# Reciprocals of token sums in two halves of the heads, each with its own store and broadcast, and their minimum and sum taken once, in a gated mix of a recurrent-memory transformer and an MLP

## The chip, the cores and the metric

The kernel runs on one core of a Trainium2 chip. The metric is the device time of one launch in microseconds (us), taken as the median of several runs. Engines are named as in the profile: PE (TensorE) with PEld, its weight loads, DVE (VectorE), ACT (ScalarE), POOL (GpSimd) and SP (SyncE), which issues most of the DMAs.

## The reference

Two branches read the same input x of 2048 tokens by 512 features, and a gate mixes them:

```python
g = _sigmoid((x * gate_w).sum(-1, keepdims=True))
a = _A_ref(x, A_mem0, A_Wq, A_Wk, A_Wv, A_Wo, A_seg_len)
b = _B_ref(x, B_w1, B_b1, B_w2, B_b2)
return g * a + (1 - g) * b
```

Branch B is a layer norm, a matmul to 1376 features, a tanh GELU and a matmul back. Branch A is a recurrence over 64 segments of 32 tokens. Each segment's input is 8 memory rows followed by its 32 tokens, 40 rows in all. The rows are projected to queries, keys and values of 32 heads with 128 features each. Scores are masked (token rows see the memory and earlier tokens, memory rows see everything), go through a softmax and weigh the values, and the output projection Wo gives 40 rows of 512. The last 32 are the segment's output, and the first 8 are the memory of the next segment. So segments cannot run side by side: each needs the 8 memory rows of the one before.

## The kernel before, in words

The whole kernel is written under a manual schedule: the order in which instructions are written is the order on each engine, and waits are derived from which tiles (and which PSUM banks) they share.

First comes branch B over 16 tiles of 128 tokens, in 8 blocks of two, while the weights of branch A are loaded. Its result, times 1 - g, goes to DRAM (`c_dr`). This takes about the first 96 us. Then comes the loop over 64 segments, `for s in range(nseg)` (L665), where s counts segments, T = s // 4 the tile of 128 tokens and si = s % 4 the place in it.

The 40 rows of a segment are split so that one matmul group has 32: 24 of its tokens with the 8 memory rows (`hT`), while the other 8 tokens ("left") of four segments are handled together for the next tile, since they don't need the memory. That left work, and the output sums, are the filler between steps of the recurrence; `run(n)` takes n pieces of it. Heads are kept as eight groups i of four, j = 0 to 3, one j for each 32 rows of the PE array. "Half 0" is the head groups i = 0 to 3, "half 1" is 4 to 7.

One segment, with the lines that the prediction uses:

- Four projections of queries and keys (L122) into the PSUM banks U, cast by ACT (L127) and transposed by DVE (L131) into QT and KT. One of the filler's is also L122, into the banks X.
- `scores` of half 0 into the bank SbF (L259, L263), one exponential on ACT (L713), values (L141, cast at L719), then the sums of half 0: `xsums` (L616) sums the exponentials of the 32 token columns into eight columns of SbF called `xs8`, and `msum` (L270, L273) sums those of the memory rows into bank U. `mnorm(0)` on DVE takes the reciprocal of the memory sums (L709, written into SbF) and multiplies it into E (L710).
- The same for half 1, in the bank W: scores, exponentials (L702, two pieces), `msum(1)`, `mnorm(1)`; later, after some filler, `xsums(E, 1)`.
- `recip_x(s)` (L625): DVE takes the reciprocal of all eight columns of `xs8` (L627) into the last eight columns of the tile R. SP stores them to DRAM (L630, 4 KB) and broadcasts them from there to all 128 partitions as `Rb` (L631, 512 KB). DVE copies the memory reciprocals into R (L633) and writes the mask into SbF again (L252). POOL adds R to the running sum `racc` (L635). DVE takes the running minimum `rmin` at the end of the segment (L766).
- `av` (L283 with the main values, L288 with the left ones): half 0 of the heads, then half 1, into the four U banks. The memory columns are cast into UT at once (L746). The token columns are copied without their normalization (`x_raw`, L622).
- `wo_pass` (L153, 32 matmuls into W) reads UT, which holds the memory columns of this segment and the normalized token columns of the segment before. `new_mem` (L659, L661) turns its result into the next segment's memory rows.
- `x_norm(s - 1)` (L638), written at the head of segment s, is where POOL multiplies the raw token columns by `Rb`: two multiplies into UT and two into UL, for each half of the heads one (L643). `Rb` has one buffer.

SP's queue holds, in program order: loads of c, VP (L182) and the transposed x at the head of a segment, then the store L630, the broadcast L631, and the stores of output tiles (L233).

`racc` and `rmin` are a check on the exponentials, which are taken without subtracting a maximum: after the loop their total over the columns (L794, L795) is compared with two limits (L797, L798), a matmul counts the partitions that are good (L810), and if one is not, a slow path recomputes branch A. With these inputs it isn't entered.

The last segment has no `xsums` and no `recip_x`. It normalizes the token columns directly with a reciprocal of 256 columns (L777) into the same tile R.

Of the kernel before, what the change touches and what calls it, by code (L numbers as in the profile page):

```python
# [27 lines left out]
def kernel(ctx, tc, A_x, A_mem0, A_Wq, A_Wk, A_Wv, A_Wo, A_seg_len, B_x, B_w1, B_b1, B_w2, B_b2, gate_w, out):  # L28
    nc = tc.nc
# [35 lines left out]
    r_dr = [dram.tile([P, NG], FP32, name=f"r_dr{i}") for i in range(2)]  # L65
# [228 lines left out]
    with tc.tile_pool(name="mlpw", bufs=1) as mlpw, \  # L294
# [44 lines left out]
        m0 = ep.tile([M, Dm], BF16)  # L339
# [228 lines left out]
    UL = [lp.tile([P, 4, NG, 32], BF16, name=f"UL{i}") for i in range(2)]  # L568
    racc = lp.tile([P, NG * 40], FP32)
# [40 lines left out]
    RW = 9 * NG  # L610
# [13 lines left out]

    def recip_x(s):  # L625
        R = Rs.pop(s)
        nc.vector.reciprocal(out=R[:, 8 * NG:RW], in_=xs8)  # L627

        Rb = cw.tile([P, P, NG], FP32, tag="Rb", bufs=1, name="Rb")
        nc.sync.dma_start(r_dr[s % 2][:], R[:, 8 * NG:RW])  # L630
        nc.sync.dma_start(Rb[:].rearrange("p r e -> p (r e)"), r_dr[s % 2][:].rearrange("r e -> (r e)").partition_broadcast(P))  # L631
# [6 lines left out]
    def x_norm(s):  # L638
        T, si = divmod(s, SPT)
        XR, Rb = XRs.pop(s), Rbs.pop(s)[:].rearrange("p (c q) (h j) -> p h j c q", c=4, h=2)  # L640
        for out, o, a, b in ((UT[(s + 1) % 2], M, LEFT, 32), (UL[T % 2], LEFT * si, 0, LEFT)):
            for h in range(2):
                nc.gpsimd.tensor_tensor(out=out[:, :, 4 * h:4 * h + 4, o:o + b - a], in0=XR[:, :, 4 * h:4 * h + 4, a:b], in1=Rb[:, h, :, :, a:b], op=ALU.mult)  # L643
# [21 lines left out]
    for s in range(nseg):  # L665
# [30 lines left out]
        R = cw.tile([P, NG * 40], FP32, tag="R", name="R")  # L696
# [26 lines left out]
        if not last:  # L723
            xsums(E, 0)
            msum(0)
            mnorm(0)
# [43 lines left out]
    nx = slice(8 * NG, 40 * NG)  # L770
    sums(xsum, E, 8, 0, 32, True)
# [5 lines left out]
    nc.vector.reciprocal(out=R[:, nx], in_=SbF[:, 0:32 * NG])  # L777
    ws[s - 1] = wo_pass(UT[s % 2])
    Rr = R[:, nx].rearrange("p (i q) -> p i q", q=32)
# [10 lines left out]
    nc.vector.tensor_tensor(out=rmin[:, nx], in0=rmin[:, nx], in1=R[:, nx], op=ALU.min)  # L790
    nc.vector.tensor_tensor(out=racc[:, nx], in0=racc[:, nx], in1=R[:, nx], op=ALU.add)
    okp = loop.enter_context(tc.tile_pool(name="okp", bufs=1))
    tot = okp.tile([P, 2], FP32)
    nc.vector.tensor_reduce(out=tot[:, 0:1], in_=rmin[:], axis=AX.X, op=ALU.min)  # L794
    nc.vector.tensor_reduce(out=tot[:, 1:2], in_=racc[:], axis=AX.X, op=ALU.add)  # L795
# [146 lines left out]
```

## Time and profile before

| what | value |
|---|---|
| median of 3 runs | 769.83 us (769.66 to 770.79) |
| span of the profiled execution | 768.4 us |
| instructions | 43822 |
| TensorE clock granted | 9 tenths or more in all 40 slices |
| DMA | 70.58 MB, mean 92 GB/s |

The span is what the profile covers of one execution; the runs' times hold a little more than that, 1.4 us by the median. "Busy" is the time in which an engine had an instruction; ends of matmuls are modelled, so the start times of matmuls say more than their ends. An idle stretch is put down to the instruction or DMA whose semaphore came last. Where an engine waits for several, the name is a guess, and it is wrong where the engine named had long been done.

### The profile page before, as it was taken

What the parts mean: (1) busy time and instruction counts of PE and PEld (TensorE: products, weight loads), DVE (VectorE), ACT (ScalarE), POOL (GpSimd) and SP (SyncE); (2) the same over time, 40 slices, a digit from 0 to 9 for tenths busy, and PEclk for the clock granted to TensorE, in tenths of its full rate; (3) what the DMA queues carried; (4) which work ended last, traced back from release to release, by engine and by line L of the source; (5) the groups of instructions that cost most, each with busy time, mean ns of one, the idle gap of its engine ahead of it and who ended that gap; (6) DMA issues with size and microseconds to landing.
All of it is one profiled execution on the core that took longest, in us unless ns stands there. A gap on an engine that the chain in (4) does not pass through costs nothing.

```text
span 768.4 us, 43822 instructions
## 1 busy us (share of the span) xinstructions
PE 753.4 (98%) x19186; PEld 412.2 (54%) x19186; DVE 396.1 (52%) x1428; ACT 540.0 (70%) x1631; POOL 278.2 (36%) x522
## 2 busy tenths in 40 slices
PE   7999999999999999999999999999999999999996
PEld 5666554555555555555555555555555555555553
DVE  5776355445445454545554554545454555444444
ACT  4666676777777777777777777777777777777763
POOL 4111033433344443334434334443424443343341
PEclk9999999999999999999999999999999999999999
DMA  6779422223222222212131322122222213122221
GB/s 196 274 233 400 153 58 63 76 63 87 65 59 66 79 72 73 80 53 74 58 89 62 90 63 79 45 80 73 80 72 59 76 49 89 62 83 64 72 67 38
DMA packets 53319, 70.58 MB, mean 92 GB/s; under 512 B 21306, under 2 KB 43043, under 8 KB 51587
## 3 DMA queue, kind: packets, MB, share of 16 engines
q1 hardware_dynamic: 51394, 64.84, 26.8%
q8 instruction: 152, 2.49, 1.4%
q0 software_dynamic: 784, 1.97, 0.8%
q10 hardware_dynamic: 944, 0.92, 0.3%
q14 instruction: 45, 0.36, 0.2%
HBM read 56.96 MB, written 4.45 MB: 80 GB/s over the span
## 4 chain that ended last, share of the span: by engine, by line
PE 96%; DMA 1%; DVE 1%; ACT 1%; issue 0%; SPq 0%; POOL 0%; DVEq 0%; ACTq 0%
PE U L122 30%; PE X L141 18%; PE W L153 15%; PE X L122 7%; PE U L468 4%; PE U L283 4%; PE X L153 4%; PE W L462 2%; PE SbF L462 2%; PE U L270 1%; PE W L259 1%; DMA w_sb<-in_B_w_dram 1%; PE U L659 1%; PE SbF L259 1%; PE SbF L616 1%; PE U L288 1%
## 5 line engine op out<-in xcount | busy, mean ns | idle before, releaser
L643 POOL TENSOR_TENSOR UT<-XR,Rb 128x384 bf16<-128x384 bf16 x126 | 140.3, 1136 | 301.7 <-DMA Rb<-r_dr 220.5
L127 ACT CAST Tb<-U 128x512 bf16<-128x512 f32 x258 | 151.2, 586 | 78.4 <-PE U L122 78.1
L122 PEld LDWEIGHTS <-hT 128*32 128x32 bf16 x4096 | 104.5, 96 | 103.9 <-DVE hT L661 8.6
L141 PE MATMUL X<-Wv_sb,hT 128*32 128x512 bf16 x2048 | 143.8, 378 | 0.0
L122 PE MATMUL U<-Wq_sb,hT 128*32 128x512 bf16 x2048 | 136.1, 381 | 0.3 <-DVE hT L661 0.2
L122 PE MATMUL U<-Wk_sb,hT 128*32 128x512 bf16 x2048 | 132.7, 379 | 0.0
L153 PE MATMUL W<-Wo_sb,UT 128*32 128x512 bf16 x2080 | 124.6, 380 | 1.2 <-POOL racc L635 1.2
L661 DVE CAST hT<-U 128x8 bf16<-128x8 f32 x126 | 20.9, 167 | 172.8 <-PE U L659 163.6
L719 ACT CAST V<-X 128x256 bf16<-128x256 f32 x256 | 88.7, 372 | 14.5 <-PE X L141 0.8
L131 DVE STREAM_TRANSPOSE QT<-Tb 128x256 f32<-128x256 f32 x128 | 57.0, 446 | 76.5 <-ACT Tb L127 76.5
L153 PEld LDWEIGHTS <-UT 128*32 128x32 bf16 x2080 | 57.8, 96 | 56.5 <-issue 13.1
L650 ACT CAST w<-W 128x128 bf16<-128x128 f32 (+1 forms) x192 | 46.0, 311 | 48.2 <-PE W L153 48.2
L622 ACT CAST XR<-U 128x256 bf16<-128x256 f32 x252 | 78.4, 434 | 0.0
L131 DVE STREAM_TRANSPOSE KT<-Tb 128x256 f32<-128x256 f32 x128 | 57.0, 445 | 28.0 <-ACT Tb L127 23.5
L643 POOL TENSOR_TENSOR UL<-XR,Rb 128x128 bf16<-128x128 bf16 x126 | 60.3, 502 | 0.0
L141 PEld LDWEIGHTS <-hT 128*32 128x32 bf16 x2048 | 46.4, 94 | 21.0
L635 POOL TENSOR_TENSOR racc<-racc,R 128x72 f32<-128x72 f32 x63 | 21.3, 338 | 93.4 <-PE U L288 84.1
L468 PE MATMUL U<-w_sb,hTm 128*128 128x512 bf16 (+1 forms) x176 | 52.4, 381 | 0.0
L746 ACT CAST UT<-U 128x64 bf16<-128x64 f32 x252 | 35.4, 226 | 22.9 <-PE U L288 22.8
L462 PEld LDWEIGHTS <-w_sb 128*128 128x128 bf16 (+1 forms) x352 | 34.5, 102 | 20.1 <-issue 1.3
L702 ACT ACTIVATE E<-W 128x64 bf16<-128x64 f32 (+1 forms) x128 | 35.0, 273 | 11.3 <-PE W L263 11.3
L659 PEld LDWEIGHTS <-w 128*32 128x32 bf16 x1008 | 22.8, 93 | 37.2 <-ACT w L650 29.3
(159 smaller groups left out, 1204.7 us busy)
## 6 DMA issues: line engine op xcount, KB each, us to landing
Rb<-r_dr SPq DMA_DIRECT2D x63, 512.0 KB, 3.8
Wv_sb<-in_A_Wv_dram SPq DMA_DIRECT2D x4, 1024.0 KB, 6.3
Wq_sb<-in_A_Wq_dram SPq DMA_DIRECT2D x4, 1024.0 KB, 7.1
Wk_sb<-in_A_Wk_dram SPq DMA_DIRECT2D x4, 1024.0 KB, 9.4
Wo_sb<-in_A_Wo_dram SPq DMA_DIRECT2D x4, 1024.0 KB, 15.0
VP<-VL SPq DMA_DIRECT2D x64, 64.0 KB, 3.5
c<-c_dr SPq DMA_DIRECT2D x16, 128.0 KB, 3.6
xt<-in_A_x_dram SPq DMA_DIRECT2D x15, 128.0 KB, 3.1
```

The lines of the kernel that those rows point to most:

```text
L122: nc.tensor.matmul(bk[32 * j:32 * j + 32, :], lhsT=G[:, kc, :], rhs=W5[t][:, kc, h0:h1, j, :], start=(kc == 0), stop=(kc == KC - 1), tile_ ...
L127: nc.scalar.copy(out=Tb[:], in_=bk.rearrange("p (a b e) -> p a e b", a=8, b=2))
L131: nc.vector.transpose(out=dst[:, 8 * hf:8 * hf + 8, c0:c0 + 32, :].rearrange("p a r b -> p a (r b)").bitcast(FP32), in_=Tb[:].rearrange("p ...
L141: nc.tensor.matmul(bk[32 * j:32 * j + 32, :], lhsT=G[:, kc, :], rhs=Wv5[:, kc, 4 * vb:4 * vb + 4, j, :], start=(kc == 0), stop=(kc == KC - ...
L153: nc.tensor.matmul(bk[32 * c:32 * c + 32, :], lhsT=U_[:, j, i, :], rhs=Wo_sb[:, 4 * i + j, :], start=(n == 0), stop=(n == NW - 1), tile_po ...
L462: nc.tensor.matmul(hp[:rows, 0:TB * P], lhsT=w1_sb[:, kc, fc * P:fc * P + rows], rhs=yTs[blk][:, kc, :], start=(kc == 0), stop=(kc == KC - 1))
L468: nc.tensor.matmul(bp(blk, tt)[:], lhsT=hTm[blk % 2][:rows, fc, tt * P:(tt + 1) * P], rhs=w2_sb[:rows, fc, :], start=(fc == 0), stop=(fc = ...
L622: nc.scalar.copy(out=XR[:, j], in_=U[j][:, 0:NG * 40].rearrange("p (i q) -> p i q", q=40)[:, :, 0:32])
L643: nc.gpsimd.tensor_tensor(out=out[:, :, 4 * h:4 * h + 4, o:o + b - a], in0=XR[:, :, 4 * h:4 * h + 4, a:b], in1=Rb[:, h, :, :, a:b], op=ALU ...
L650: nc.scalar.copy(out=w[:, a:b], in_=W[:, a:b])
L719: nc.scalar.copy(out=V[:, i0:i0 + 2, :].rearrange("p i e -> p (i e)"), in_=(X1, X2)[vb][:, 256 * h:256 * h + 256])
L746: nc.scalar.copy(out=UT[s % 2][:, j, :, 0:M], in_=U[j][:, 0:NG * 40].rearrange("p (i q) -> p i q", q=40)[:, :, 32:40])
```

## The change

R loses the eight columns for the token sums. A new tile RX keeps the reciprocals of all 63 segments, eight columns each. They are taken in two pieces: half 0 right after `msum(0)`, ahead of `mnorm(0)` on DVE, and half 1 where L627 was. Each piece has its own store to its own DRAM tile, and each DRAM tile its own broadcast into its own `Rb` tile; both broadcasts are written in `recip_x`, behind the second store. The running sum and minimum keep the 64 columns of memory sums alone; those of the token sums are taken once after the loop, with two reductions over all 504 columns of RX, and they join the check as second operands of its two comparisons. The reciprocal of the last segment gets a tile of its own. One small tile (m0) moves to the pool of branch B.

```diff
-    r_dr = [dram.tile([P, NG], FP32, name=f"r_dr{i}") for i in range(2)]
+    r_dr = [[dram.tile([P, NG // 2], FP32, name=f"r_dr{i}{h}") for h in range(2)] for i in range(2)]
...
-        m0 = ep.tile([M, Dm], BF16)
+        m0 = mlpw.tile([M, Dm], BF16)
...
+    RX = lp.tile([P, nseg - 1, NG], FP32)
...
-    RW = 9 * NG
+    RW = 8 * NG
...
+    def recip_half(s, h):
+        r = RX[:, s, 4 * h:4 * h + 4]
+        nc.vector.reciprocal(out=r, in_=xs8[:, 4 * h:4 * h + 4])
+        nc.sync.dma_start(r_dr[s % 2][h][:], r)
+
     def recip_x(s):
+        recip_half(s, 1)
         R = Rs.pop(s)
-        nc.vector.reciprocal(out=R[:, 8 * NG:RW], in_=xs8)
-
-        Rb = cw.tile([P, P, NG], FP32, tag="Rb", bufs=1, name="Rb")
-        nc.sync.dma_start(r_dr[s % 2][:], R[:, 8 * NG:RW])
-        nc.sync.dma_start(Rb[:].rearrange("p r e -> p (r e)"), r_dr[s % 2][:].rearrange("r e -> (r e)").partition_broadcast(P))
+        Rb = []
+        for h in range(2):
+            Rb.append(cw.tile([P, P, NG // 2], FP32, tag=f"Rb{h}", bufs=1, name="Rb"))
+            nc.sync.dma_start(Rb[h][:].rearrange("p r e -> p (r e)"), r_dr[s % 2][h][:].rearrange("r e -> (r e)").partition_broadcast(P))
...
-        XR, Rb = XRs.pop(s), Rbs.pop(s)[:].rearrange("p (c q) (h j) -> p h j c q", c=4, h=2)
+        XR, Rb = XRs.pop(s), [r[:].rearrange("p (c q) j -> p j c q", c=4) for r in Rbs.pop(s)]
...
-                nc.gpsimd.tensor_tensor(out=out[:, :, 4 * h:4 * h + 4, o:o + b - a], in0=XR[:, :, 4 * h:4 * h + 4, a:b], in1=Rb[:, h, :, :, a:b], op=ALU.mult)
+                nc.gpsimd.tensor_tensor(out=out[:, :, 4 * h:4 * h + 4, o:o + b - a], in0=XR[:, :, 4 * h:4 * h + 4, a:b], in1=Rb[h][:, :, :, a:b], op=ALU.mult)
...
-        R = cw.tile([P, NG * 40], FP32, tag="R", name="R")
+        R = cw.tile([P, RW], FP32, tag="R", name="R")
...
             xsums(E, 0)
             msum(0)
+            recip_half(s, 0)
             mnorm(0)
...
+    okp = loop.enter_context(tc.tile_pool(name="okp", bufs=1))
+    R = okp.tile([P, 32 * NG], FP32)
+    tot = okp.tile([P, 2, 2], FP32)
+    xr = RX[:].rearrange("p s e -> p (s e)")
+    nc.vector.tensor_reduce(out=tot[:, 0, 0:1], in_=xr, axis=AX.X, op=ALU.min)
+    nc.vector.tensor_reduce(out=tot[:, 1, 0:1], in_=xr, axis=AX.X, op=ALU.add)
...
-    nc.vector.reciprocal(out=R[:, nx], in_=SbF[:, 0:32 * NG])
+    nc.vector.reciprocal(out=R[:], in_=SbF[:, 0:32 * NG])
...
-    nc.vector.tensor_scalar(out=good[:, 0:1], in0=tot[:, 0:1], scalar1=R_MIN, scalar2=None, op0=ALU.is_gt)
-    nc.vector.tensor_scalar(out=good[:, 1:2], in0=tot[:, 1:2], scalar1=RSUM_MAX, scalar2=None, op0=ALU.is_lt)
+    nc.vector.tensor_scalar(out=good[:, 0:1], in0=tot[:, 0, 1:2], scalar1=tot[:, 0, 0:1], scalar2=R_MIN, op0=ALU.min, op1=ALU.is_gt)
+    nc.vector.tensor_scalar(out=good[:, 1:2], in0=tot[:, 1, 1:2], scalar1=tot[:, 1, 0:1], scalar2=RSUM_MAX, op0=ALU.add, op1=ALU.is_lt)
```

12 lines of the change are left out of this document (5 added, 7 removed).

## The prediction

> **What bounds the kernel now.** I read the page first: busy time by engine, then the chain that ended last.
>
> ```profile
> PE 753.4 (98%) x19186; PEld 412.2 (54%) x19186; DVE 396.1 (52%) x1428; ACT 540.0 (70%) x1631; POOL 278.2 (36%) x522
> ```
> ```profile
> PE 96%; DMA 1%; DVE 1%; ACT 1%; issue 0%; SPq 0%; POOL 0%; DVEq 0%; ACTq 0%
> ```
>
> TensorE is the bound. The edit touches VectorE, GpSimd, SyncE's queue and DMA, so it can change the time only where one of these ends a wait of TensorE. Next come the waits: GpSimd's largest, then the two of TensorE's that lie in the loop.
>
> ```profile
> POOL UT L643 <- DMA Rb<-r_dr: 220.5, 45, 6.2
> ```
> ```profile
> PE U L659 <- ACT w L650: 1.5, 4, 0.4
> PE W L153 <- POOL racc L635: 1.2, 3, 0.4
> ```
>
> The change works on the first of these, 220.5 us of GpSimd waiting for the broadcast `Rb`. It is large, but TensorE is not waiting behind it: its only wait that names GpSimd is 1.2 us in 3 places. A busy TensorE hides short stalls, since ends of matmuls are modelled, so I went on to the start times of one segment of 10 us, by engine: VectorE, ScalarE, TensorE, GpSimd, and SyncE's queue.
>
> ```profile
> 401.51 0.37 DVE L709 RECIPROCAL SbF<-U 128x32 f32<-128x32 f32 x1 [0.34 <-ACT V L719]
> 401.91 0.22 DVE L710 TENSOR_TENSOR E<-E,SbF 128x64 bf16<-128x64 bf16 x1
> 402.37 0.37 DVE L709 RECIPROCAL W<-U 128x32 f32<-128x32 f32 x1 [0.24 <-ACT E L702]
> 402.77 0.22 DVE L710 TENSOR_TENSOR E<-E,W 128x64 bf16<-128x64 bf16 x1
> 402.97 0.21 DVE L627 RECIPROCAL R<-SbF 128x8 f32<-128x8 f32 x1
> ```
> ```profile
> 402.02 0.32 ACT L702 ACTIVATE E<-W 128x160 bf16<-128x160 f32 x1
> ```
> ```profile
> 401.10 0.20 PE L616 MATMUL SbF<-BO,E 128*32 128x4 bf16 x8
> 401.15 0.18 PE L270 MATMUL U<-E,BO 128*32 128x32 bf16 x4
> 401.18 0.18 PE L273 MATMUL U<-E,BO 128*32 128x32 bf16 x4
> ...
> 402.77 0.30 PE L283 MATMUL U<-E,V 32*128 32x40 bf16 x16
> 402.89 0.21 PE L288 MATMUL U<-E,VP 32*128 32x64 bf16 x4
> 403.05 0.29 PE L283 MATMUL U<-E,V 32*128 32x40 bf16 x16
> ...
> 403.77 1.91 PE L153 MATMUL W<-Wo_sb,UT 128*32 128x512 bf16 x32
> ```
> ```profile
> 399.78 2.24 POOL L643 TENSOR_TENSOR UT<-XR,Rb 128x384 bf16<-128x384 bf16 x2 [5.97 <-DMA Rb<-r_dr]
> ```
> ```profile
> 403.21 0.33 SPq L630 DMA_DIRECT2D r_dr<-R  x1
> 404.66 0.32 SPq L631 DMA_DIRECT2D Rb<-r_dr  x1
> 405.07 0.53 SPq L182 DMA_DIRECT2D VP<-VL  x1
> ```
>
> Columns: start, duration, engine, line, then in brackets the idle time and what ended it. Two things are to be seen. First, the attention-times-V matmuls follow VectorE closely: the first L283 starts at 402.77, 0.03 after the second L709 reciprocal ends (402.37 + 0.37 = 402.74), the second at 403.05, 0.06 after the second L710 multiply ends (402.99). So **the second normalization sets TensorE's pace, and it starts 0.03 after ScalarE's exponential ends** (402.02 + 0.32 = 402.34). Ahead of it VectorE idled 0.24. Second, GpSimd's `UT` is done at 402.02 and read at 403.77: **1.75 us of reserve**. The tightest segment that I found:
>
> ```profile
> 452.09 2.23 POOL L643 TENSOR_TENSOR UT<-XR,Rb 128x384 bf16<-128x384 bf16 x2 [6.15 <-DMA Rb<-r_dr]
> ```
> ```profile
> 455.25 1.91 PE L153 MATMUL W<-Wo_sb,UT 128*32 128x512 bf16 x32
> ```
>
> Here 455.25 - 454.32 = 0.93 us are left. The broadcast is never what TensorE waits for in this execution.
>
> **The change part by part.** The sum is made against the profiled execution's span, 768.4 us; the median of the runs shown is 769.83, so 1.4 us lie around the span and I add them unchanged. There are 63 segments with the changed work (the last has none).
>
> ```profile
> L709 DVE RECIPROCAL W<-U 128x32 f32<-128x32 f32 x63 | 23.1, 367 | 16.3 <-ACT E L702 12.0 <-PE X L141 3.9 <-PE U L273 0.4
> ...
> L627 DVE RECIPROCAL R<-SbF 128x8 f32<-128x8 f32 x63 | 13.1, 207 | 0.1
> ```
>
> 1. *The reciprocal of half 0, added ahead of the first L709.* 24 columns fewer take 160 ns less (367 to 207), 6.7 ns a column, so four columns take about 180 ns; bounds 0 and the 367 of the 128x32 row, and 207 is the nearest. It reads the L616 sums, which leave TensorE 0.05 to 0.08 before the L273 sums that the first L709 waits for, so it starts about 0.05 earlier than 401.51. The first L709 writes the same bank and waits for its end, plus the 0.03 seen between L709 and L710 (401.88 to 401.91). Queued behind it on VectorE are both normalizations. They move by 0.18 + 0.03 - 0.05 = 0.16 (0.19 with 207). The second L709 had 0.24 idle here and 16.3 / 63 = 0.26 in the mean, and its start is set by ScalarE. Cost **0**; 0.05 to 0.08 of cover remain, and each 10 ns beyond cost 0.63 us. The matmuls of half 1's sums also wait for the first L710, whose end moves to about 402.3; they come after the second L709 has started.
>
> 2. *The reciprocal of half 1*, in the place of L627: four columns for eight, 27 ns less, behind the second normalization, with nothing of TensorE behind it soon. 0. Its old wait for GpSimd moves to the copy that follows; the instruction waited for is two segments old.
>
> 3. *Two stores and two broadcasts* instead of one each, all on SyncE's queue in the order store 0, store 1, broadcast 0, broadcast 1.
>
> ```profile
> r_dr<-R SPq DMA_DIRECT2D x63, 4.0 KB, 1.5
> ```
> ```profile
> DMA to landing us min/median/max: 3.3/3.8/5.6
> ```
>
> Store 0 can go at about 401.7 and lands by 403.2; store 1 goes at 403.2 as before; broadcast 0 at about 403.5 instead of 404.66; broadcast 1 at 404.7, when store 1 has landed. Half 0 arrives about 1.1 us earlier, half 1 with half the bytes at about the old time. 63 x 2 more DMAs take 0.33 of SyncE's queue each; behind them stands the VP load (405.07), which the next segment needs some 10 us after the L288 at 402.89, so a third of a us there costs nothing. GpSimd's four multiplies keep their sizes; two may start earlier, into 1.75 us of reserve that nobody uses. Gain **0**. [...] The 4 KB store here lands in 1.5, and SyncE issues the VP load 0.41 after the broadcast, long before that has landed. [...]
>
> 4. *Minimum and sum once at the end.* L635 on GpSimd and L766 on VectorE lose 8 of 72 columns each; neither has TensorE behind it. Two reductions over 504 columns are added before the last reciprocal:
>
> ```profile
> 752.76 0.45 DVE L131 STREAM_TRANSPOSE KT<-Tb 128x256 f32<-128x256 f32 x1 [0.36 <-ACT Tb L127]
> 755.05 1.76 DVE L777 RECIPROCAL R<-SbF 128x256 f32<-128x256 f32 x1 [1.85 <-ACT V L719]
> ...
> 760.62 0.47 DVE L795 TENSOR_REDUCE tot<-racc 128x1 f32<-128x320 f32 x1
> ```
>
> In proportion 0.47 x 504 / 320 = 0.74 each, 1.5 together, within 1.85 of idle. Uncovered they would cost at most 1.5 once. The two checks keep their number; a second operand from memory in each is 0 within hundredths. Cost 0. The two tiles that move in memory change no wait that is still open when it is reached.
>
> **Sum**: 768.4 + 0 + 1.4 = **769.8 us**.
>
> **The rivals.**
>
> *VectorE becomes late (slower).* If the added reciprocal holds the first L709 for more than 0.24, the second L709 starts late, and L283 with it. At the upper bound, 0.37 + 0.03 - 0.05 = 0.35, so 0.11 x 63 = 6.9: 776.7. For it: the chain is tight and repeated 63 times. Against: the 128x8 reciprocal took 0.21.
>
> *The pair of broadcasts lands later (slower).* Two transfers share one queue and have packets half as long. If each pair ended as late as the slowest broadcast of this trace, 5.6 instead of 3.8, `UT` would be 1.8 later, 0.05 beyond the reserve of 1.75, times 62 = 3.1: 772.9. It decides from 0.93 late in the tightest segment on. Against: half 1's transfer is half as large.
>
> *The irregular stalls go (faster).* Every fourth segment has the same work, so equal spacing is expected. The chain in order of time:
>
> ```profile
> 106.81 3.45 PE U L122 x64
> ...
> 604.50 3.45 PE U L122 x64
> ...
> 645.75 3.45 PE U L122 x64
> ```
>
> Four segments took 41.25 at 604.50, but 497.69 / 12 = 41.47 before that: 12 x 0.22 = 2.7 us of irregular stalls, the 1.2 after GpSimd among them. If the new timing removed all, 767.1. Nothing ties them to the broadcast: `UT` was ready 0.93 or more ahead.
>
> *The change doesn't do what it says*: broadcast 0 stands behind store 1 in the queue, and if it then waits on as before, nothing arrives earlier. The time is again 769.8, since earliness is not used.
>
> **How the numbers follow.** Forecast, with the last rival in it, 0.74, its own range 768.3 to 771.3; the stalls go 0.10; late broadcasts 0.08; late VectorE 0.08. The bound for no change is 0.2%, about 1.5 us, roughly what a measurement of this kernel can tell. Faster 0.10, same 0.74, slower 0.16. The range from 768.3 to 772.9 takes in the forecast and the late broadcasts, 0.82.
>
> **What would show it.** Right: the second L709 still starts 0.03 after L702 ends, its idle falls from 0.26 to about 0.1, L283 keeps its place, GpSimd's wait for `Rb` falls from 220.5 by some 40 to 70 while TensorE's busy time stays near 753, four clean segments take 41.25. Wrong: idle before the second L709 gone and named by VectorE itself, a `UT` that ends after its L153 could start, the KT transpose to last reciprocal stretch at the end longer, or four clean segments off 41.25 by more than 0.1.

## The result and the profile after

The changed kernel took 778.19 us in the median (776.17 to 779.33, 4 runs) beside 770.31 for the kernel before (4 runs): a ratio of 1.0093, 95% interval 1.0074 to 1.0112. Run once more, later, it took 779.30 (1.0107, 1.0090 to 1.0123). It is slower by about 8 us, where 769.8 was forecast and 772.9 was the upper end. The profiled span went from 768.4 to 776.3 us.

Of the changed kernel's page, the lines that answer to those of before: busy time by engine, the chain by engine, and of the DMA queues SyncE's (q1) and the one that brings instructions (q8; packets, MB, share of the time of the 16 DMA engines).

```profile
PE 759.4 (98%) x19186; PEld 418.7 (54%) x19186; DVE 407.0 (52%) x1493; ACT 539.7 (70%) x1631; POOL 278.1 (36%) x522
...
q1 hardware_dynamic: 69538, 64.85, 31.3%
q8 instruction: 152, 2.49, 1.6%
...
PE 95%; DVE 2%; ACT 1%; issue 1%; DMA 1%; POOL 0%; DVEq 0%; ACTq 0%; POOLq 0%
```

The same two queues in the kernel before:

```profile
q1 hardware_dynamic: 51394, 64.84, 26.8%
q8 instruction: 152, 2.49, 1.4%
```

TensorE has the same 19186 matmuls and is "busy" 6.0 us longer (753.4 to 759.4). The change gave it no more work, so this busy time holds pauses too short or too unlike a wait to be shown as idle. The bytes on q1 are equal to 0.01 MB, but they come in a third more packets and hold the DMA engines for 31.3% of the span instead of 26.8%; the instruction queue, with the same 152 packets, went from 1.4 to 1.6%.

The waits of the changed kernel that the change touches (engine, tile and line, what it waited for: us in total, times, longest):

```profile
POOL UT L649 <- DMA Rb<-r_dr: 254.9, 101, 5.2
...
POOL UT L649 <- ACT Tb L127: 27.2, 7, 4.7
...
DVE RX L628 <- PE U L273: 18.2, 62, 0.6
...
ACT E L708 <- DVE RX L628: 10.2, 52, 0.2
...
PEld L122 <- issue: 4.0, 9, 0.6
...
PE W L153 <- ACT UT L753: 1.2, 3, 0.4
```

And in the kernel before:

```profile
POOL UT L643 <- ACT Tb L127: 81.2, 18, 5.9
...
PEld L122 <- issue: 1.8, 5, 0.4
```

GpSimd's wait for `Rb` did not fall, it rose by 34 us; what fell is its wait for `Tb` (81.2 to 27.2), so that both together went from 301.7 to 282.1. The wait changed its name more than its size. Two lines stand out. ScalarE's exponentials now name the added reciprocal. And TensorE's weight loads of L122, in the middle of the projection, sat longer behind "issue", a wait for nothing that the profile shows: 4.0 us in 9 places instead of 1.8 in 5.

One segment of the changed kernel by start times, first VectorE, ScalarE and TensorE around the normalizations:

```profile
404.53 0.20 PE L617 MATMUL SbF<-BO,E 128*32 128x4 bf16 x8
...
404.89 0.18 DVE L628 RECIPROCAL RX<-SbF 128x4 f32<-128x4 f32 x1 [0.55 <-PE U L273]
...
405.11 0.22 ACT L708 ACTIVATE E<-W 128x64 bf16<-128x64 f32 x1 [0.20 <-DVE RX L628]
405.18 0.37 DVE L715 RECIPROCAL SbF<-U 128x32 f32<-128x32 f32 x1
...
405.48 0.32 ACT L708 ACTIVATE E<-W 128x160 bf16<-128x160 f32 x1
405.58 0.22 DVE L716 TENSOR_TENSOR E<-E,SbF 128x64 bf16<-128x64 bf16 x1
...
405.84 0.36 DVE L715 RECIPROCAL W<-U 128x32 f32<-128x32 f32 x1
...
406.23 0.29 PE L283 MATMUL U<-E,V 32*128 32x40 bf16 x16
```

The second L715 starts 0.04 after ScalarE's exponential (405.48 + 0.32 = 405.80) and 0.04 after VectorE's own multiply, which ends at 405.80 too. Before, VectorE had been free 0.24 earlier. From the start of the sums' matmuls (404.53) to the second reciprocal it takes 1.31 here; it took 1.27 before (401.10 to 402.37).

SyncE's queue in that segment, GpSimd's multiplies ahead of it, and the pass that reads `UT`:

```profile
405.10 1.81 SPq L629 DMA_DIRECT2D r_dr<-RX  x2
...
407.02 2.79 SPq L637 DMA_DIRECT2D Rb<-r_dr  x2
...
409.87 0.54 SPq L182 DMA_DIRECT2D VP<-VL  x1
```
```profile
400.28 1.12 POOL L649 TENSOR_TENSOR UT<-XR,Rb 128x384 bf16<-128x384 bf16 x1 [3.46 <-DMA Rb<-r_dr]
400.38 1.10 DVE L773 TENSOR_TENSOR rmin<-rmin,R 128x64 f32<-128x64 f32 x1
...
402.22 1.13 POOL L649 TENSOR_TENSOR UT<-XR,Rb 128x384 bf16<-128x384 bf16 x1 [0.82 <-DMA Rb<-r_dr]
...
403.30 0.28 PE L259 MATMUL SbF<-QT,KT 128*32 128x40 bf16 x16
```
```profile
407.27 1.91 PE L153 MATMUL W<-Wo_sb,UT 128*32 128x512 bf16 x32
```

`UT` is ready at 403.35 and read at 407.27: 3.9 us of reserve, where the segment of the prediction had 1.75. This segment gains more than most. Over all 63 the median reserve went from 2.8 to 3.1 us and the smallest from 0.9 to 1.8, and nobody uses it. The two broadcasts did not come as planned either: counted from the last sums matmul of half 0, the first is issued at 2.78 us and the second at 4.84 (medians), where the single one was at 3.63. The first is earlier, the second later. And one row says what was not foreseen: the running minimum L773 beside GpSimd's first multiply took 1.10 us; alone it takes 0.22. The groups show that this is no rule of the kernel but a few places:

```profile
L715 DVE RECIPROCAL SbF<-U 128x32 f32<-128x32 f32 x63 | 23.1, 366 | 7.0 <-DVE RX L628 0.8
L715 DVE RECIPROCAL W<-U 128x32 f32<-128x32 f32 x63 | 23.0, 366 | 3.3 <-ACT E L708 0.8 <-PE U L273 0.3
L628 DVE RECIPROCAL RX<-SbF 128x4 f32<-128x4 f32 x126 | 22.9, 182 | 18.9 <-PE U L273 18.2 <-PE W L263 0.6
...
L773 DVE TENSOR_TENSOR rmin<-rmin,R 128x64 f32<-128x64 f32 x63 | 17.2, 273 | 0.1
```

The last row, 63 minima with a mean of 273 ns, is 3.3 us more than 63 x 0.22; it sits in five minima, one of 0.51 and four of 0.98 to 1.10 (in the kernel before, all 63 took 0.22 within a few ns). The second row is the idle time before the second reciprocal: 3.3 / 63 = 0.05, where 0.26 was before.

The chain in order of time, at a stretch of four segments among the cleanest:

```profile
169.48 3.55 PE U L122 x64
...
210.89 3.55 PE U L122 x64
```

41.41 us for four segments; the cleanest four took 41.36, where clean groups of four repeat at 41.25 before (some at both ends of the loop took less). The regular cost is therefore about 0.11 / 4 x 63 = 1.7 us. The rest of the 8 us is irregular. In the time line TensorE shows it as pauses in the middle of a group:

```profile
522.00 0.21 PE L288 MATMUL U<-E,VP 32*128 32x64 bf16 x3 [0.61 <-issue]
```
```profile
564.06 0.23 PE L283 MATMUL U<-E,V 32*128 32x40 bf16 x9 [0.56 <-issue]
```

The last 3 of L288's matmuls and the last 9 of L283's come 0.6 us late, with no semaphore to wait for: their operands were there for the first ones of the same group. I listed each start-to-start gap of over 0.235 us between matmuls (128 to 725 us of the trace) ahead of which no instruction of TensorE waits for a semaphore: 4 in the kernel before, 13 in the changed one, 21 in its second run (the expectations below speak of 2 in the kernel before; this bound gives 4). **All of them stand at the same place in TensorE's instruction stream, counted modulo 256** (the 193rd to 195th; the 180th to 182nd in traces where 13 matmul records are missing), and 1.2 to 1.6 us after the end of a 16384-byte packet on q8. TensorE's 19186 matmuls and 19186 weight loads make 150 blocks of 256, and q8, whose kind the page gives as "instruction", carried 152 such packets: about one packet for each 256 instructions. So I read a pause as TensorE at the end of the instructions it has, waiting for the next block of 256. That is my reading of place and time; no trace shows which instructions TensorE has at hand.

So three theories stood beside each other for the 8 us: **A**, the chain through the added reciprocal; **B**, the minimum that is stretched beside GpSimd and holds the transposes behind it; **C**, instruction blocks that come late because of the two broadcasts.

### The profile page after: what moved, and what is told of

The parts are those of the page before. It is cut to its first block, busy times and chain, and to the rows that moved or that the text cites. A ratio compares the mean times of both kernels' runs of the same rounds, so it can differ in the third digit from the quotient of the medians.

```text
span 776.3 us, 44095 instructions
## 1 busy us (share of the span) xinstructions
PE 759.4 (98%) x19186; PEld 418.7 (54%) x19186; DVE 407.0 (52%) x1493; ACT 539.7 (70%) x1631; POOL 278.1 (36%) x522
## 3 DMA queue, kind: packets, MB, share of 16 engines
q1 hardware_dynamic: 69538, 64.85, 31.3%
## 4 chain that ended last, share of the span: by engine, by line
PE 95%; DVE 2%; ACT 1%; issue 1%; DMA 1%; POOL 0%; DVEq 0%; ACTq 0%; POOLq 0%
PE U L122 29%; PE X L141 18%; PE W L153 15%; PE X L122 7%; PE U L468 5%; PE U L283 4%; PE X L153 4%; PE W L462 2%; PE SbF L462 2%; PE U L270 1%; PE W L259 1%; PE U L665 1%; PE SbF L259 1%; PE SbF L617 1%; DMA b1r<-in_B_b_dram 1%
## 5 line engine op out<-in xcount | busy, mean ns | idle before, releaser
L649 POOL TENSOR_TENSOR UT<-XR,Rb 128x384 bf16<-128x384 bf16 x126 | 142.2, 1132 | 285.5 <-DMA Rb<-r_dr 254.9
L122 PEld LDWEIGHTS <-hT 128*32 128x32 bf16 x4096 | 106.5, 96 | 103.7 <-DVE hT L667 8.5
L141 PE MATMUL X<-Wv_sb,hT 128*32 128x512 bf16 x2048 | 145.6, 378 | 0.0
L122 PE MATMUL U<-Wq_sb,hT 128*32 128x512 bf16 x2048 | 138.5, 381 | 0.4 <-DVE hT L667 0.2
L122 PE MATMUL U<-Wk_sb,hT 128*32 128x512 bf16 x2048 | 134.5, 379 | 0.0
L641 POOL TENSOR_TENSOR racc<-racc,R 128x64 f32<-128x64 f32 x63 | 20.1, 319 | 116.1 <-PE U L288 104.3
L141 PEld LDWEIGHTS <-hT 128*32 128x32 bf16 x2048 | 49.6, 94 | 20.1 <-issue 0.2
L649 POOL TENSOR_TENSOR UL<-XR,Rb 128x128 bf16<-128x128 bf16 x126 | 60.0, 499 | 0.0
L708 ACT ACTIVATE E<-W 128x64 bf16<-128x64 f32 (+1 forms) x128 | 35.0, 273 | 13.4 <-DVE RX L628 10.2
```

The source lines that it names most:

```text
L122: nc.tensor.matmul(bk[32 * j:32 * j + 32, :], lhsT=G[:, kc, :], rhs=W5[t][:, kc, h0:h1, j, :], start=(kc == 0), stop=(kc == KC - 1), tile_ ...
L141: nc.tensor.matmul(bk[32 * j:32 * j + 32, :], lhsT=G[:, kc, :], rhs=Wv5[:, kc, 4 * vb:4 * vb + 4, j, :], start=(kc == 0), stop=(kc == KC - ...
```

## The experiments

Each ran beside the kernel before on the same chip; "1.0034 (1.0021 to 1.0048)" is the ratio to it with its 95% interval. The names e1 to e17 are used in the expectations.

### e1, e2, e3: the first reciprocal moved, the minimum moved, both

On the changed kernel. e1:

```
             msum(0)
-            recip_half(s, 0)
             mnorm(0)
+            recip_half(s, 0)
```

e2, and e3 is both:

```
         mask_put(0)
+        nc.vector.tensor_tensor(out=rmin[:, 0:RW], in0=rmin[:, 0:RW], in1=R[:, 0:RW], op=ALU.min)
         nc.gpsimd.tensor_tensor(out=racc[:, 0:RW], in0=racc[:, 0:RW], in1=R[:, 0:RW], op=ALU.add)
...
-        nc.vector.tensor_tensor(out=rmin[:, 0:RW], in0=rmin[:, 0:RW], in1=R[:, 0:RW], op=ALU.min)
```

> The changed kernel with the reciprocal of half 0 put behind mnorm(0) on VectorE instead of ahead of it. Theory chain (the reciprocal ahead of mnorm(0) makes the second normalization start 0.03 later in each of 63 segments, some 2 of the 7.9 us): 2.0 us less than the changed kernel, about 776.2, and VectorE idles about 0.05 to 0.25 again before the second L715. Theory instruction fetch (the additional DMA packets hold up the fetch of TensorE's instructions, some 4 us) and theory clash (rmin on VectorE stands behind GpSimd's multiplies, which now start earlier, some 1 to 2 us): no change beyond 1 us, about 778.

> The changed kernel with the running minimum of the segment moved from the segment's end to recip_x, right behind the mask, where GpSimd has no large multiply. Theory clash: the minimum takes 0.22 us in every segment instead of about 1.0 in five of them, and the time falls by 1 to 2 us, to about 776.5. Theories chain and instruction fetch: about 778, whatever the minimum takes.

> The changed kernel with both moves. Chain and clash together: 3 to 4 us less, about 774.5, and the rest of 4 us over the kernel before stays, since two stores and two broadcasts stay. If chain and clash were the whole cause: 770.3.

Measured: e1 774.97 us, 1.0060 (1.0038 to 1.0081); e2 772.89, 1.0034 (1.0021 to 1.0048); e3 772.26, 1.0033 (1.0021 to 1.0046).

A is confirmed in its mechanism. Instruction by instruction, from the start of the last sums matmul, medians of 63 segments: first multiply done 0.996 before, 1.228 changed, 0.994 in e1; first exponential 0.511, 0.536, 0.509; second exponential done 1.206, 1.231, 1.204; second reciprocal 1.238, 1.265, 1.237; first L283 1.634, 1.657, 1.633. The added reciprocal eats all of VectorE's cover and also puts the exponential 0.025 later; moved behind the first normalization, both are back. 0.023 x 63 = 1.5 us by the medians. The means give between 0.030 and 0.037, by which matmul of the sums one counts from; with 0.035 it is 2.2, the term used below. Clean groups of four segments say the same: 41.36 in e2, e5 and e13, which have the added reciprocal ahead, and 41.25 in e1, e3 and e7. But e1 gained 3.2 us by the medians, more than this and more than was expected, so something else moved with it too. Why the exponential, which reads another bank, follows the added reciprocal was not settled.

B seemed confirmed by e2, which gains 0.6% on the changed kernel and has all 63 minima at 0.21 to 0.22:

```profile
L641 DVE TENSOR_TENSOR rmin<-rmin,R 128x64 f32<-128x64 f32 x63 | 13.6, 216 | 0.0
```

But that gain of some 5 us is more than the 3.3 us by which the minima were too long, and the parts do not add: moving the reciprocal as well (e3 on e2) gains 0.6 by the medians, where A should have given 1.5 or more. e2 and e3 came out 3.6 and 2.2 below what was expected of them. Something else had changed with them.

### e4, e9: two broadcasts alone

On the kernel before. e4 with two stores, e9 with one store of both halves:

```
-        Rb = cw.tile([P, P, NG], FP32, tag="Rb", bufs=1, name="Rb")
-        nc.sync.dma_start(r_dr[s % 2][:], R[:, 8 * NG:RW])
-        nc.sync.dma_start(Rb[:].rearrange("p r e -> p (r e)"), r_dr[s % 2][:].rearrange("r e -> (r e)").partition_broadcast(P))
+        for h in range(2):
+            nc.sync.dma_start(r_dr[s % 2][h][:], R[:, 8 * NG + 4 * h:8 * NG + 4 * h + 4])
+        Rb = []
+        for h in range(2):
+            Rb.append(cw.tile([P, P, NG // 2], FP32, tag=f"Rb{h}", bufs=1, name="Rb"))
+            nc.sync.dma_start(Rb[h][:].rearrange("p r e -> p (r e)"), r_dr[s % 2][h][:].rearrange("r e -> (r e)").partition_broadcast(P))
```

> The kernel before with two stores and two broadcasts of half the size, all issued where it issued its one store and one broadcast; one reciprocal of eight columns, nothing else changed. Theory instruction fetch: 3 to 5 us more than the kernel before, about 774, by irregular pauses of TensorE in the middle of matmul groups that wait for nothing named. Theories chain and clash: 770.3, as the kernel before.

> The kernel before with one store (into a DRAM tile laid out by halves) and two broadcasts of half the size. Against the two stores and two broadcasts alone, 3.7 us over the kernel before: if the broadcasts are the cause, 3 to 4 over before, 773 to 774; if it is the second store, about as before, 770 to 771.

e4: 773.73, 1.0049 (1.0032 to 1.0066). e9: 776.71, 1.0079 (1.0057 to 1.0101). With VectorE's work untouched, cutting the broadcast alone costs 3.7 to 6 us. It is the broadcasts and not the second store, since e9 has only one store and is no faster; that it is slower than e4, and 2.7 above its range, was not foreseen and is not explained.

### e5, e7, and the changed kernel again: one broadcast, and the end part alone

e5 is the changed kernel with both reciprocals and stores, into one DRAM tile, and one broadcast of 512 KB; e7 has one reciprocal and store as well, so that only the reductions at the end are left of the change:

```
-        nc.sync.dma_start(r_dr[s % 2][h][:], r)
+        nc.sync.dma_start(r_dr[s % 2][:, 4 * h:4 * h + 4], r)
...
-        Rb = []
-        for h in range(2):
-            Rb.append(cw.tile([P, P, NG // 2], FP32, tag=f"Rb{h}", bufs=1, name="Rb"))
-            nc.sync.dma_start(Rb[h][:].rearrange("p r e -> p (r e)"), r_dr[s % 2][h][:].rearrange("r e -> (r e)").partition_broadcast(P))
+        Rb = cw.tile([P, P, NG], FP32, tag="Rb", bufs=1, name="Rb")
+        nc.sync.dma_start(Rb[:].rearrange("p r e -> p (r e)"), r_dr[s % 2][:].rearrange("r e -> (r e)").partition_broadcast(P))
```

> The changed kernel with its two reciprocals and two stores, but one DRAM tile (the stores write alternating pieces of 16 B) and one broadcast of 512 KB as before. Theory DMA packets, if the broadcasts of 2 KB pieces are what holds up instruction fetch: 3 to 4 us less than the changed kernel; and since the multiplies start as late as before, no minimum behind them, another 1 to 2 less: 771 to 773, with the chain's 2 us left. If the stores' small pieces are the cause: 775 to 777.

> The changed kernel with one reciprocal of eight columns, one store and one broadcast: what is left of the change is the tile that keeps all reciprocals, the shorter running minimum and sum, and the two reductions at the end. All theories: as the kernel before, 769.5 to 770.5; anything over 771.5 would mean a cause in the end or in the memory layout that none of them has.

> The changed kernel itself, timed again beside the next ones on one chip. All theories: 776 to 778, and it serves as the mark for the others.

e5: 774.39, 1.0047 (1.0035 to 1.0059). e7: 771.64, 1.0011 (0.9999 to 1.0024). Changed kernel: 779.30. The end part costs nothing that can be told from zero, though e7 lies 0.14 above the 771.5 that was to mark an unknown cause. e5 has the late reciprocal in full and none of the stretched minima, and lies clearly between. It lies between its two expectations as well and bears out neither.

### e8: the clash by itself

The kernel before, with the minimum of a segment put to where GpSimd's multiplies of the next one run:

```
+            if n == 2 and s >= 1:
+                nc.vector.tensor_tensor(out=rmin[:, 0:RW], in0=rmin[:, 0:RW], in1=Rl[:, 0:RW], op=ALU.min)
...
-        nc.vector.tensor_tensor(out=rmin[:, 0:RW], in0=rmin[:, 0:RW], in1=R[:, 0:RW], op=ALU.min)
+        Rl = R
```

> The kernel before with the running minimum of a segment moved to behind the third query/key transpose of the next segment, where GpSimd's multiplies of x_norm run; the minimum of the last segment is left out of the guard. Theory (VectorE's instruction with two SBUF inputs is stretched beside a GpSimd multiply and holds up what is behind it): the minimum takes about 1.0 us instead of 0.22 in most of the 62 segments, and where it does, transposes of the next segment come late and TensorE waits 0.3 to 0.8 us: 20 to 50 us in all, 790 to 820 us. Rival (the stretched minimum costs VectorE alone, and the five in the changed kernel are beside the path): below 772 us.

776.60, 1.0096 (1.0071 to 1.0122): between the two expectations, and a miss for both. The group of the minimum, and the wait of TensorE that it makes:

```profile
L695 DVE TENSOR_TENSOR rmin<-rmin,R 128x72 f32<-128x72 f32 x63 | 32.9, 523 | 0.0
```
```profile
PE W L259 <- DVE KT L131: 3.8, 12, 0.5
```

42 of the minima took over 0.3 us, 19 us in all above 63 x 0.22, and the time rose by 6.3: about 0.15 for each. The stretch is real and reaches the path, but at that price the five of the changed kernel are worth some 0.8 us (an estimate from this run, for another place in the segment). So e2's gain was mostly something else.

### e10, e11, e12, e6: what in the broadcasts

e10 is e7 with the reciprocals in bf16 (one broadcast of 256 KB in pieces of 2 KB). e11 cuts the broadcast of the kernel before by destination partitions, e12 lays it out so that one broadcast has 256 pieces of 2 KB, e6 sends a second whole one to a tile that nobody reads:

The edits of e10 (with the same for `r_dr` and `Rb`), e11, e12 and e6:

```
-    RX = lp.tile([P, nseg - 1, NG], FP32)
+    RX = lp.tile([P, nseg - 1, NG], BF16)
```
```
-        nc.sync.dma_start(Rb[:].rearrange("p r e -> p (r e)"), r_dr[s % 2][:].rearrange("r e -> (r e)").partition_broadcast(P))
+        for k in range(2):
+            nc.sync.dma_start(Rb[64 * k:64 * k + 64].rearrange("p r e -> p (r e)"), r_dr[s % 2][:].rearrange("r e -> (r e)").partition_broadcast(64))
```
```
-    r_dr = [dram.tile([P, NG], FP32, name=f"r_dr{i}") for i in range(2)]
+    r_dr = [dram.tile([2, P * NG], FP32, name=f"r_dr{i}") for i in range(2)]
...
+        rd = r_dr[s % 2][:, 0:P * NG // 2]
+        nc.sync.dma_start(rd.rearrange("h (r e) -> r h e", e=NG // 2), R[:, 8 * NG:RW].rearrange("p (h e) -> p h e", h=2))
+        nc.sync.dma_start(Rb[:], rd.partition_broadcast(P))
```
```
         nc.sync.dma_start(Rb[:].rearrange("p r e -> p (r e)"), r_dr[s % 2][:].rearrange("r e -> (r e)").partition_broadcast(P))
+        Qb = cw.tile([P, P, NG], FP32, tag="Qb", bufs=1, name="Qb")
+        nc.sync.dma_start(q_dr[s % 2][:], R[:, 8 * NG:RW])
+        nc.sync.dma_start(Qb[:].rearrange("p r e -> p (r e)"), q_dr[s % 2][:].rearrange("r e -> (r e)").partition_broadcast(P))
```

> The kernel of e7 (end reductions alone: 771.6 us, 1.0011 of before) with the reciprocals, their DRAM tile and Rb in bf16: one store, one broadcast of 256 KB in pieces of 2 KB in place of 512 KB in pieces of 4 KB. Theory: two broadcasts delay the fetch of TensorE's instructions because their pieces are half as long (2 KB). Then the slow fetches (over 1.6 us; 3 in e7, 21 in the kernel with the pairs alone) are back, 10 or more, and the time is 773 to 775 us. Rival 1: it is the number of transfers or their bytes, not the length of a piece; then at most 5 slow fetches and 770 to 772 us. Rival 2: the shorter broadcast and GpSimd's multiplies on 2-byte operands free something that the path needs: below 769 us.

> The kernel before with its broadcast cut in two by destination partitions (64 each) instead of by heads: two transfers of 256 KB, pieces of 4 KB as before, one store. Theory (length of the pieces): at most 6 slow fetches, 770 to 771 us. Rival (number of broadcasts): 12 or more slow fetches and 773 to 777 us, as with two broadcasts by heads (773.7 and 776.7).

> The kernel before with a second store of the reciprocals and a second broadcast of 512 KB per segment into a tile that nothing reads: twice the bytes and twice the packets, pieces of 4 KB. Theory (length of the pieces): the slow fetches stay at most 6 and the time 770 to 772 us, though the DMA share of the queue rises to about 31% or more. Rival (bytes or number of packets on the rings that instruction fetch shares): 12 or more slow fetches, 773 us or more.

> The kernel before with its DRAM tile and Rb laid out in two halves of the heads, but still one store and one broadcast of 512 KB: 256 pieces of 2 KB where it had 128 of 4 KB. So far: two transfers with 128 pieces of 4 KB cost nothing (770.2), one of 256 KB in 128 pieces of 2 KB nothing (769.8), two of 256 KB in 256 pieces of 2 KB 3.7 to 6 us. Theory (number of pieces per segment): 773 to 776 us, queue share 30% or more, pauses of TensorE without a named wait 8 or more. Rival (two transfers at once of short pieces are needed): 770 to 771 us, pauses as before (2).

e10: 769.78, 1.0001 (0.9990 to 1.0013). e11: 770.24, 1.0002 (0.9992 to 1.0012). e12: 769.89, 1.0007 (0.9995 to 1.0018). e6: 820.07, 1.0650 (1.0611 to 1.0690).

My first reading of C falls. I had taken slow q8 packets (over 1.6 us in the loop; 4 in the kernel before, 28 in the changed one) for the cause, and short pieces for the cause of those. e10 and e12 have short pieces and 17 and 12 slow packets and lose nothing; e6 has none and loses 50 us. Neither two transfers (e11), nor 256 pieces (e12), nor pieces of 2 KB (e10, e12) cost by themselves. What does separate the free kernels from the others is **how long per segment broadcast packets are under way**: 2.0 us in e10, 2.6 in the kernel before and e12, 2.9 in e11, all free; 3.1 in e9, 3.3 in e4, 3.6 in the changed kernel, 5.1 in e6. It does not order those that cost something: e9 costs more than e4.

### e13, e14, e15: the account

e13 is e5 with the minimum moved as in e2; e14 the changed kernel with bf16 broadcasts, e15 the same on e3.

> The changed kernel with one broadcast of 512 KB and the running minimum ahead of GpSimd's sum: of the three causes the later second reciprocal alone (0.03 us a segment, 2 us, and the end part's 0.8). If it adds up: 772 to 773.5 us. If the reciprocal's chain costs more than its mean shows (the kernel with one broadcast alone gave 774.4): 774 us or more. If it is hidden and what was read as chain was something else: 771 or less.

> The changed kernel with reciprocals, DRAM tiles and Rb in bf16: two broadcasts of 128 KB in 256 pieces of 1 KB per segment, half the bytes. Chain and clash stay. Theory (time on the rings): queue share about 26%, pauses without a named wait as before (2 to 5), the part of the broadcasts (2.5 to 4 us) goes: 773.5 to 776 us. Rival (number of pieces): pauses stay 10 or more, 777 to 780 us.

> The changed kernel with all three causes taken away and its two reciprocals, two stores, two broadcasts and end reductions kept: the first reciprocal behind the first normalisation, the minimum ahead of GpSimd's sum, and bf16 broadcasts. If the three close the account: 770 to 771.7 us, as the end reductions alone (771.6 in f32, 769.8 in bf16). If a fourth is open: 773 us or more.

e13: 771.70, 1.0029 (1.0018 to 1.0040). e14: 783.73, 1.0172 (1.0148 to 1.0195). e15: 778.52, 1.0126 (1.0107 to 1.0146). e13 came a little below what was expected of the chain alone. e14 and e15 are clear misses: half the bytes in pieces of 1 KB made the two broadcasts dearer. Their packets are under way as long or longer (3.9 and 3.6 us per segment), and TensorE shows it where the changed kernel did (e14):

```profile
PEld L122 <- issue: 6.5, 15, 1.1
```

### e16, e17: the same transfers, close together or apart

e10 with a second bf16 store and broadcast to a tile that nobody reads. In e17 both stores stand ahead of both broadcasts; in e16 the second store stands behind the first broadcast, so that the second broadcast waits for it. Only the order of four issues differs. e16, and then what e17 changes in it:

```
         nc.sync.dma_start(Rb[:].rearrange("p r e -> p (r e)"), r_dr[s % 2][:].rearrange("r e -> (r e)").partition_broadcast(P))
+        Qb = cw.tile([P, P, NG], BF16, tag="Qb", bufs=1, name="Qb")
+        nc.sync.dma_start(q_dr[s % 2][:], RX[:, s, :])
+        nc.sync.dma_start(Qb[:].rearrange("p r e -> p (r e)"), q_dr[s % 2][:].rearrange("r e -> (r e)").partition_broadcast(P))
```
```
         nc.sync.dma_start(r_dr[s % 2][:], r)
+        nc.sync.dma_start(q_dr[s % 2][:], RX[:, s, :])
...
-        nc.sync.dma_start(q_dr[s % 2][:], RX[:, s, :])
```

> The kernel of e10 (end reductions alone, one bf16 broadcast of 256 KB, 769.8 us, stretch of the broadcast 2.0 us) with a second store and a second bf16 broadcast of 256 KB per segment into a tile that nothing reads, issued behind the first broadcast, so that the second waits for its own store and begins some 2 us after the first: as many bytes and pieces as e12 (512 KB in 256 pieces of 2 KB, 769.9 us, stretch 2.6 us). The broadcast that GpSimd reads is no later. Theory (the stretch in which broadcast packets hold the rings decides, from about 3 us on, since TensorE's instruction block then comes late): stretch 4 us or more, pauses of TensorE without a named wait 10 or more, 775 to 785 us. Rival (bytes or pieces decide): 770 to 771 us. If the second pair holds SyncE's queue up instead, TensorE waits by name for the transfer of VP.

> The same transfers as in the kernel with the second pair staggered, but both stores are issued first and both broadcasts behind them. Theory (stretch): 2.6 to 3.2 us of broadcast packets per segment, so 769.5 to 773 us, at least 3 us under the staggered one. Rival (two transfers of short pieces cost by themselves, however they lie): both alike, 773 us or more.

e17: 772.96, 1.0046 (1.0030 to 1.0061). e16: 798.88, 1.0391 (1.0354 to 1.0429). The bytes, the pieces and the transfers are the same, the order alone makes 26 us. The direction is as the theory had it, the size was under-estimated. Part of the 26 has another cause: in e16 SyncE's queue, where the second broadcast waits for its store, also holds up the VP load, and TensorE names it; the rest is named "issue":

```profile
PE U L289 <- DMA VP<-VL: 6.5, 7, 1.4
PE U L284 <- issue: 5.9, 7, 1.2
PE W L154 <- issue: 4.2, 7, 1.2
```

### The account over all runs

For each of TensorE's some 130 blocks of 256 instructions between 128 and 725 us I read two things from the trace: whether the block's first instruction comes within 1.65 us of the end of the q8 packet before it (a block used as soon as it is there: "late"), and how long the gap at that instruction is, summed where it is over 0.15 us. The last columns are the profiled span less 768.4, and the sum of two terms: the gaps less the 5.0 of the kernel before, and 2.2 for the later second reciprocal in the kernels that have it. e6 and e8 are not in it: e6 follows below the table, and e8, with one broadcast, has 6% late blocks, so its loss is not of this kind.

| kernel | broadcasts per segment | packets under way, us | late blocks | gaps, us | span - 768.4 | gaps + chain |
|---|---|---|---|---|---|---|
| before | 1, 128 x 4 KB | 2.6 | 19% | 5.0 | 0 | 0 |
| e10 | 1, 128 x 2 KB | 2.0 | 12% | 4.4 | -1.2 | -0.6 |
| e12 | 1, 256 x 2 KB | 2.6 | 21% | 4.7 | -0.8 | -0.3 |
| e11 | 2, 128 x 4 KB | 2.9 | 21% | 5.5 | 0.4 | 0.5 |
| e7 | 1, 128 x 4 KB | 2.5 | 20% | 6.8 | 1.8 | 1.8 |
| e13 (chain) | 1, 128 x 4 KB | 2.5 | 15% | 4.6 | 0.3 | 1.8 |
| e5 (chain) | 1, 128 x 4 KB | 2.7 | 21% | 7.2 | 3.3 | 4.4 |
| e3 | 2, 256 x 2 KB | 3.4 | 27% | 6.5 | 1.6 | 1.5 |
| e1 | 2, 256 x 2 KB | 3.5 | 27% | 7.3 | 2.0 | 2.3 |
| e2 (chain) | 2, 256 x 2 KB | 3.6 | 24% | 5.4 | 1.8 | 2.6 |
| e17 | 2, 256 x 2 KB | 3.3 | 32% | 8.5 | 2.2 | 3.5 |
| e4 | 2, 256 x 2 KB | 3.3 | 29% | 8.2 | 2.9 | 3.2 |
| e9 | 2, 256 x 2 KB | 3.1 | 29% | 9.3 | 4.7 | 4.3 |
| changed (chain) | 2, 256 x 2 KB | 3.6 | 40% | 10.2 | 7.9 | 7.4 |
| changed, again (chain) | 2, 256 x 2 KB | 3.7 | 47% | 13.3 | 11.7 | 10.5 |
| e15 | 2, 256 x 1 KB | 3.6 | 41% | 12.8 | 7.8 | 7.8 |
| e14 (chain) | 2, 256 x 1 KB | 3.9 | 54% | 15.7 | 13.2 | 12.9 |
| e16 | 2, 256 x 2 KB | 3.9 | 33% | 25.6 | 28.7 | 20.6 |

For all but e16 the two terms give the span within 1.5 us; of e16's other 8 us, 6.5 are the wait for the VP load. e6 has gaps of 24.1 and 12.6 us of that wait, and in its loop TensorE's granted clock fell to 0.5 four times for 3.41 us (at 127, 458, 503 and 550 us), an estimated 6.8 us more (half of 4 x 3.41), of its 41.8 in all. So C carries most of the change: in the profiled run 5.2 of the 7.9 us are gaps at the blocks' first instructions, read as blocks that come later, 1.5 to 2.2 are the chain, and what is left for the clash and the end part is about 1 us. None of the terms is sharper than 1 or 2 us: e7, with one broadcast as before, has 1.8 us more of gaps, and two runs of the changed kernel differ by 3.1.

That the blocks come later beside the broadcasts can be read from the traces more directly, though these are blocks at different places of a segment. From the boundary at which TensorE begins one block I took the start of the q8 packet that brings the next. In the kernel before it starts 0.71 us after the boundary, in the mean, where less than 0.1 us of the first 2 us has broadcast packets under way, and 1.59 after it where more than 1 us has; in the changed kernel 0.91 and 1.99. All 20 traces have it this way round. The end of the packet comes, in the mean over all blocks, 2.06 us after the boundary in the kernel before, 2.4 to 2.5 in e1 to e4, e9 and e17, and 2.7 to 3.0 in the two runs of the changed kernel, e14 and e15. In e6 and e16, which lose most, it is no later than 2.6.

Three things stay open. Packets under way for over 3 us go with late blocks in every run, but they don't set how many: e1, e2 and e3 have the broadcasts of the changed kernel, 3.4 to 3.6 us, and 24 to 27% late blocks where the changed kernel has 40 and 47; why the place of a VectorE minimum or reciprocal matters to that was not found. Nor does the distance between the two broadcasts explain it, as e16 and e17 suggest: they are issued 0.4 us apart in e9, which loses 6 us, and 1.8 apart in e2, which loses 2.6 with the chain in it (medians of 63 segments; 0.5 in e17, 4.1 in e16). And whether a block is late because its packet starts late or runs slowly was seen both ways: slow packets in the changed kernel (mean 1.27 us, 1.12 before), quick but late ones in e6 (mean 1.02). How the two kinds of packets share the DMA engines or rings, of which some expectations speak, no run here shows.

None of the kernels beats the one before beyond its interval; e10, the nearest, is 1.0001 (0.9990 to 1.0013).

## Why the prediction was wrong

**Step 1, cost 0: wrong in a term, small in size.** The reciprocal's own length was right (about 180 ns estimated, 182 measured), and so was its start: 0.32 after the last matmul of `xsums`, in the median, where the first L709 had started 0.374 after it. The failed term is the 0.03 added for the next start. It was taken from a pair (L709 to L710), and this pair shows 0.11: 405.07 to 405.18 in the rows above, 7.0 / 63 = 0.11 in the group. So the normalization moved by 0.23, not 0.16, and of the cover of 0.24 nothing was left; with the exponential 0.025 later as well, the second reciprocal starts 0.03 later. Cost 1.5 to 2.2 us instead of 0, and "four clean segments" went off by 0.11, the sign that the prediction had named. The rival *VectorE becomes late* was this mechanism, with 6.9 as its price at the 367 ns bound; its 776.7 lies near the result for another reason.

**Step 2, the reciprocal of half 1: right**, nothing is seen of it.

**Step 3, gain or cost 0: here the prediction failed.** Its reading of the path was right: `UT` is never late, with 3.1 us of reserve in the median where it was 2.8, and what GpSimd gains is unused. But it priced the DMAs only by who waits for their data. Beside their packets those of q8 start later (1.59 us after a block's boundary, 0.71 without them), and that showed in the trace of before, had I looked: four pauses with no name, all at a block's boundary, and a median of 2.5 us between a block's arrival and its use (1.8 in the changed kernel). The wait view calls such time "issue", and I had set down the 2.7 us of irregular stalls as tied to nothing. e4 and e9, which change the broadcasts alone, put 3.7 to 6 us on this step. The store's median landing rose from 1.5 to 2.2, and the second broadcast was issued 1.2 us later than the single one had been, not at about the same time, as the step has it; but neither landing is on the path.

Of the same step, "two may start earlier, into 1.75 us of reserve that nobody uses" missed what the earlier multiply meets: VectorE's minimum, 0.51 to 1.10 instead of 0.22 in five segments. That was an instruction that took longer beside GpSimd's (0.43 to 1.02 of each of the five lies beside an L649), not a wait, and no row of before showed it: all 63 minima took 0.22 there. By e8 it is worth some 0.8 us. Why the minimum takes longer beside a multiply no run shows.

**Step 4, the end: right within what can be measured** (e7, 1.0011, 0.9999 to 1.0024). The second operand of the two checks, forecast as 0 within hundredths, made each 0.05 to 0.06 us longer: 0.20 and 0.21 where they had taken 0.14 and 0.16.

The rival *pair of broadcasts lands later* is refuted as a cost by the reserve, 1.8 us at the least, though the second broadcast does go later, *irregular stalls go* by their growth, and *the change doesn't do what it says* by GpSimd's first multiply, which starts after the first half alone. The forecast that GpSimd's wait for `Rb` would fall by 40 to 70 was wrong in the wait's name: waits for `Rb` and `Tb` together fell by 19.6.

## What to carry to other kernels

On an engine that is always busy, a cost can hide in its busy time (753.4 and 759.4 us here, for the same 19186 matmuls): compare busy totals at equal instruction counts, and look where gaps without a named wait stand in the instruction stream. A transfer off the critical path was not free here where instruction packets travelled beside it (3.7 us in e4, 6 in e9); send in one transfer what can be sent in one (e12, 769.89 us, is free where e4, 773.73, and e9, 776.71, are not), and count the issues behind it on the same queue (the VP load, 6.5 us of waiting in e16). A cover of some hundredths of a us is no cover where it is eaten sixty times (0.03 x 63, 1.5 to 2.2 us here); price it with the gap of the very pair of instructions, or let the range hold it.

## What the runs showed of the hardware

- All 4 unnamed gaps of TensorE in the kernel before, 13 and 21 of the changed kernel, 9 of e4, 20 of e14 and 23 of e16 stand at one position of its instruction stream modulo 256 (within three instructions), 1.2 to 1.6 us after the end of a 16384-byte packet on q8; q8 carried 152 of these for 150 times 256 instructions. Where the profile names the gaps at all, it is as "issue". That TensorE waits there for its next block of instructions is a reading of this.
- In the kernel before such a packet started 0.71 us after the boundary before it where hardly any broadcast packets were under way and 1.59 where they were for over half of 2 us; 0.91 and 1.99 in the changed kernel.
- The same two bf16 broadcasts and their stores cost 3 us close together and 29 us staggered (e17 772.96, e16 798.88), 6.5 of the 29 as a wait for a load held up behind them.
- Two broadcasts in pieces of 1 KB cost more than two with twice the bytes in pieces of 2 KB (e14 783.7, changed kernel 778 to 779).
- A 128x64 f32 minimum of two tensors in memory took up to 1.10 us beside a GpSimd multiply and 0.22 alone.
- From the end of the added 128x4 reciprocal to the start of the next one passed 0.11 us; from a reciprocal to the multiply that reads its result, 0.03.
